# One PSUM ring, v projected ahead of k, q kept for the first attention block, attention in four stages between the FFN's tiles

## The chip, the cores and the metric

One core of a Trainium2 chip. The time is device microseconds of one execution of the program; the profile is one execution recorded by the hardware profiler. The engines are TensorE (PE), VectorE (DVE), ScalarE (ACT), GpSimd (POOL) and SyncE (SP, which only issues loads and stores here; ACT issues some too). Each engine runs its own queue in order, and waits on semaphores for the others.

## The reference

A transformer block over x of 2048 rows by 640: linear attention with a learned softmax feature map (32 heads of 20), then a gated FFN of 1536, both behind a layernorm and with a residual. All arrays are bf16.

```python
qkv = split(layernorm(x) @ wqkv)                    # q, k, v: 32 heads of 20
pq, pk = q @ w_phi[h], k @ w_phi[h]                 # 20 x 20 for each head
phi_q = concat(softmax(pq), softmax(-pq))
phi_k = concat(softmax(pk), softmax(-pk))
kv, z = sum_s(phi_k * v), sum_s(phi_k)
o = (phi_q @ kv) / (phi_q @ z + 1e-6)
h = x + o @ wo
out = h + (gelu(layernorm(h) @ w_gate) * (layernorm(h) @ w_up)) @ w_down
```

## The kernel before

The 2048 rows are 16 tiles of 128 rows, in 4 blocks of 4 tiles. The kernel has two phases, each with its own SBUF and PSUM pools.

Phase 1 (lines 93 to 281). `fold` multiplies w_phi into the weights of k and q (`Wk2`, `Wq2`): it transposes the raw weights piece by piece (tile `tp`, copied to `WT`), and multiplies each by block diagonals `BD` (L149, L156, PSUM `wa` and `wb`). `ln1` normalises a tile, transposes it on PE (L169) and stores it in `LN1T`. For each tile `k_tile` projects k (L183, PSUM `pk`), takes exp(pk) and exp(-pk) on ACT (`E`, L187), sums them by head on DVE (`sk`, L190) and takes reciprocals (`rs`, L192). `v_tile`, one tile behind, projects v (L200, `pv`), and scales it by `rs` into `vt`: one sign on DVE out of PSUM (L206), the other on POOL out of an SBUF copy `vS` (L210), with a column of `rs` (L213). `kv_half` sums over 8 tiles (L223, `kvp`); its second run adds the first half (`acc`) and masks into `KV` (L232, L233). `q_chunk` projects one 128-column piece of q for a block (L243, `pq`) and takes both exps into `Eq`: 20 chunks, from tile 6 on one per tile, the rest behind the second `kv_half`.

Phase 2 (from L286). Its pools open when phase 1 is over, and its weights `Wg`, `Wu`, `Wd` are loaded then. `attn(b, tl)` handles one tile: 14 matmuls of `Eq` with `KV` (L313, `ab`), ACT copies to `AB` (L320), then a chain on DVE: `pr`, `den`, `rd`, two `w`, two `tt` (L333, L336), `o` (L340). PE transposes o (L343, `tpo`), ACT copies it to `oT`, PE multiplies by `Wo` (L350, `po`), DVE adds x into `h_b` (L352), takes statistics, POOL computes `ve` and `rstd` (L87, L89), DVE writes `ln` (L356), PE transposes it (L359, `tpl`) and ACT copies it to `LN2T`. `ffn(b)` has 12 steps of gate and up (L367, L371; gelu on ACT, product `GT` on DVE), then for each of 4 tiles 24 matmuls of down (L381, `pd`), the residual on DVE (`y`, L384) and a store. The program writes attn(0, 0..3), then for each block attn of the next block and ffn of this one.

The order on each engine is not quite that of the code: the framework's scheduler moves instructions forward where their operands allow, within the buffers that the pools hold. PSUM in phase 2 is five one-bank buffers for `ab`, `gp`, `up`, two for `po` and `pd`, one for transposes.

Of the kernel before, what the change touches and what calls it, by code (L numbers as in the profile page):

```python
# [17 lines left out]
def kernel(  # L18
# [50 lines left out]
    nhalf = const.tile([P, 1], F32, name="nhalf")  # L69

    mid_cm = tc.tile_pool(name="mid", bufs=1, side="right")
    mid = mid_cm.__enter__()
    LN1T = [mid.tile([P, NC, 512], BF16, name=f"LN1T{b}") for b in range(NB)]
    Wq2 = mid.tile([P, NC, D], BF16, name="Wq2")
# [4 lines left out]
    def ln_stats(pool, halves, tag):  # L79

        stats = small(pool, [P, 2, nc.vector.BN_STATS_DIM], "stats" + tag)
        for i, hv in enumerate(halves):
            nc.vector.bn_stats(stats[:, i, :], hv)  # L83
        mv = small(pool, [P, nc.vector.BN_AGGR_DIM], "mv" + tag)
        nc.vector.bn_aggr(mv, stats)  # L85
        ve = small(pool, [P, 1], "ve" + tag)
        nc.gpsimd.tensor_scalar_add(ve, mv[:, 1:2], EPS)  # L87
        rstd = small(pool, [P, 1], "rstd" + tag)
        nc.gpsimd.tensor_tensor(rstd, ve, nhalf, op=ALU.pow)  # L89
        return mv, rstd  # L90


    with tc.tile_pool(name="p1", bufs=1) as p1, \
            tc.tile_pool(name="p1t", bufs=1, space=PSUM) as psT, \
            tc.tile_pool(name="p1k", bufs=1, space=PSUM) as psK, \
            tc.tile_pool(name="p1v", bufs=1, space=PSUM) as psV, \
            tc.tile_pool(name="p1q", bufs=2, space=PSUM) as psQ, \
            tc.tile_pool(name="p1a", bufs=1, space=PSUM) as psA:
        raw_k = p1.tile([P, NC, D], BF16, name="raw_k")
# [24 lines left out]
        nc.gpsimd.affine_select(out=m6, in_=m6, pattern=[[Dh, 6]], compare_op=ALU.is_ge,
                                fill=0.0, base=Dh - 1, channel_multiplier=-1)

        nc.vector.tensor_tensor(
            BD[0:120, 0:5], wphi[0:120, 0:5, None, :].to_broadcast([120, 5, 6, Dh]),
            m6[0:120, None, :, None].to_broadcast([120, 5, 6, Dh]), ALU.mult)
        nc.vector.tensor_tensor(  # L130
            BD[0:40, 5, 0:2], wphi[0:40, 5, None, :].to_broadcast([40, 2, Dh]),
            m6[0:40, 0:2, None].to_broadcast([40, 2, Dh]), ALU.mult)

        def fold(raw, W2):

            WT = p1.tile([P, 6, D], BF16, name="WT", bufs=1)
            for g, (o, n) in enumerate(FG):
                tp = psT.tile([P, NC, P], BF16, name="tp", tag="T")
                for c in range(NC):
                    nc.tensor.transpose(tp[0:n, c, :], raw[:, c, o:o + n], ident)  # L140
                if g % 2 == 0:
                    nc.vector.tensor_copy(WT[0:n, g, :], tp[0:n])
                else:
                    nc.scalar.copy(WT[0:n, g, :], tp[0:n])
            for c in range(NC):
                wa = psQ.tile([P, 512], F32, name="wa", tag="Q")
                for g in range(4):
                    o, n = FG[g]
                    nc.tensor.matmul(wa[:, o:o + n], lhsT=WT[0:n, g, c * P:(c + 1) * P],  # L149
                                     rhs=BD[0:n, g].rearrange("p a b -> p (a b)")[:, 0:n],  # L150
                                     start=True, stop=True)
                nc.scalar.copy(W2[:, c, 0:480], wa[:, 0:480])
                wb = psQ.tile([P, 512], F32, name="wb", tag="Q")
                for g in range(4, 6):
                    o, n = FG[g]
                    nc.tensor.matmul(wb[:, o - 480:o - 480 + n], lhsT=WT[0:n, g, c * P:(c + 1) * P],  # L156
                                     rhs=BD[0:n, g].rearrange("p a b -> p (a b)")[:, 0:n],
                                     start=True, stop=True)
                nc.vector.tensor_copy(W2[:, c, 480:640], wb[:, 0:160])

        def ln1(t):
            b, tl = divmod(t, 4)
            xt = x_sb[b][:, tl, :]
            mv, rstd = ln_stats(p1, [xt[:, 0:HD], xt[:, HD:D]], "1")
            ln = p1.tile([P, D], BF16, name="ln", bufs=3)
            nc.vector.tensor_scalar(ln, xt, mv[:, 0:1], rstd, op0=ALU.subtract, op1=ALU.mult)
            tp = psT.tile([P, NC, P], BF16, name="tp", tag="T")
            for c in range(NC):
                nc.tensor.transpose(tp[:, c, :], ln[:, c * P:(c + 1) * P], ident)  # L169
# [255 lines left out]
```

## Time and profile before

| | us |
|---|---|
| median of 3 runs | 373.04 (371.33 to 373.2) |
| the profiled execution, its own time | 372.27 |
| its span, first to last instruction | 370.2 |
| PE busy in the span | 313.7 (85%) |
| DVE busy | 206.0 (56%) |
| ACT busy | 148.6 (40%) |
| POOL busy | 58.7 (16%) |
| mean granted PE clock | 0.945 |

How to read it: a row of the stages gives each engine's busy time in a stretch; a row of the waits gives who idled for whom. PE's busy time is inflated where the granted clock is low, since the same matmul then takes longer. The chain that ended last consists of PE for 61% and of DVE for 22%.

### The profile page before, as it was taken

The page shows a single profiled execution, that of the slowest core. Times are in us where ns is not written, and L with a number is a line of the kernel's source. Part 1 is how long each engine was busy: PE and PEld are TensorE (multiplying, and loading weights), DVE is VectorE, ACT ScalarE, POOL GpSimd, SP SyncE. Part 2 cuts the span into 40 slices and gives each one's busy share as a digit, 9 for nine tenths or more (in the row PEclk, how much of TensorE's full clock was granted, in tenths as well). Part 3 has the DMA queues.
Part 4 walks back from the last instruction along what each step waited for, and adds up shares of the span by engine and source line. Part 5 has one row for each costly group of instructions (what it writes and reads, how often), then busy time and mean ns, then how long its engine had stood idle before and what let it go on. Part 6 is the DMA issues. An engine that isn't in the chain of part 4 may idle for free.

```text
span 370.2 us, 5473 instructions
## 1 busy us (share of the span) xinstructions
PE 313.7 (85%) x2163; PEld 191.1 (52%) x2188; DVE 206.0 (56%) x454; ACT 148.6 (40%) x260; POOL 58.7 (16%) x121
## 2 busy tenths in 40 slices
PE   0278999999999765468899979989988989999996
PEld 0156766776665443234445754444764444754464
DVE  4728899546652877835443277743359743332232
ACT  1056877778767542332431054233045233013200
POOL 4604365324410000001000001010001010000000
PEclk9989999999999866559999989999999999999999
DMA  8900000000004930000000100000010000010001
GB/s 262 372 6 4 2 0 3 0 2 2 0 0 123 397 122 1 0 2 0 0 3 0 55 18 2 0 0 2 35 38 0 2 0 3 35 37 0 0 19 54
DMA packets 9202, 14.79 MB, mean 40 GB/s; under 512 B 1113, under 2 KB 7385, under 8 KB 9177
## 3 DMA queue, kind: packets, MB, share of 16 engines
q1 hardware_dynamic: 6544, 11.96, 9.1%
q10 hardware_dynamic: 2633, 2.48, 2.0%
q8 instruction: 17, 0.28, 0.3%
q14 instruction: 8, 0.07, 0.1%
HBM read 11.82 MB, written 2.62 MB: 39 GB/s over the span
## 4 chain that ended last, share of the span: by engine, by line
PE 61%; DVE 22%; ACT 5%; DMA 4%; issue 4%; POOL 4%; ACTq 0%; POOLq 0%; DVEq 0%
PE pd L381 14%; PE gp L367 9%; PE up L371 9%; PE po L350 5%; PE pv L200 4%; PE pk L183 4%; DVE stats L83 4%; DMA Wv<-in_A_wqkv_dram 4%; PE pq L243 4%; PE kvp L223 3%; DVE h_b L352 3%; POOL rstd L89 2%; DVE ln L356 2%; DVE sk L190 2%; PE tpl L359 2%
## 5 line engine op out<-in xcount | busy, mean ns | idle before, releaser
L367 PE MATMUL gp<-LN2T,Wg 128*128 128x512 bf16 x229 | 61.9, 386 | 0.9 <-issue 0.4
L371 PE MATMUL up<-LN2T,Wu 128*128 128x512 bf16 x236 | 60.9, 379 | 0.2
L374 ACT ACTIVATE g<-gp 128x512 bf16<-128x512 f32 x48 | 28.7, 598 | 79.8 <-PE gp L367 74.0
L375 DVE TENSOR_TENSOR GT<-up,g 128x512 bf16<-128x512 f32 x48 | 32.8, 684 | 43.9 <-PE up L371 43.9
L381 PE MATMUL pd<-Wd,GT 128*128 128x320 bf16 x384 | 52.8, 299 | 0.0
L381 PEld LDWEIGHTS <-GT 128*128 128x128 bf16 x384 | 37.6, 98 | 15.2
L87 POOL TENSOR_SCALAR ve<-mv 128x1 f32<-128x1 f32 x32 | 7.9, 250 | 210.7 <-DVE mv L85 185.0
L320 ACT COPY AB<-ab 128x484 f32<-128x484 f32 (+1 forms) x48 | 23.0, 569 | 38.1 <-PE ab L313 27.5
L371 PEld LDWEIGHTS <-Wu 128*128 128x128 bf16 x240 | 23.3, 98 | 25.5
L367 PEld LDWEIGHTS <-Wg 128*128 128x128 bf16 x240 | 23.4, 99 | 24.2 <-issue 1.1
L384 DVE TENSOR_TENSOR y<-pd,h_b 128x320 bf16<-128x320 f32 x32 | 15.7, 492 | 35.3 <-PE pd L381 35.3
L350 PE MATMUL po<-Wo,oT 128*128 128x320 bf16 x160 | 31.8, 360 | 2.4 <-ACT oT L345 2.4
L200 PE MATMUL pv<-Wv,LN1T 128*128 128x320 bf16 x160 | 26.5, 309 | 3.9 <-DMA Wv<-in_A_wqkv_dram 2.9
L190 DVE TENSOR_REDUCE sk<-E 128x64 f32<-128x1280 bf16 x16 | 23.7, 1479 | 9.2 <-ACT E L187 9.1
L183 PE MATMUL pk<-Wk,LN1T 128*128 128x320 bf16 x160 | 26.4, 301 | 1.1 <-ACT E L187 1.1
L350 PEld LDWEIGHTS <-oT 128*128 128x128 bf16 x160 | 17.3, 115 | 17.0 <-ACT oT L345 7.7
L360 ACT COPY LN2T<-tpl 128x640 bf16<-128x640 bf16 x16 | 11.1, 692 | 37.1 <-PE tpl L359 37.1
L352 DVE TENSOR_TENSOR h_b<-po,x_sb 128x320 bf16<-128x320 f32 x32 | 15.4, 485 | 17.7 <-PE po L350 17.4
L359 PE MATMUL tpl<-ident,ln 128*128 128x128 bf16 x80 | 8.0, 238 | 19.3 <-DVE ln L356 19.3
L210 POOL TENSOR_TENSOR vt<-vS,rs 128x640 bf16<-128x640 bf16 x16 | 20.4, 1273 | 24.6 <-ACT vS L204 20.9
L243 PE MATMUL pq<-LN1T,Wq 128*128 128x512 bf16 x90 | 23.6, 379 | 0.4
L187 ACT ACTIVATE E<-pk 128x640 bf16<-128x640 f32 x32 | 21.0, 702 | 6.6 <-PE pk L183 6.2
(72 smaller groups left out, 400.6 us busy)
## 6 DMA issues: line engine op xcount, KB each, us to landing
out_dram<-y SPq DMA_DIRECT2D x16, 160.0 KB, 1.8
x_sb<-in_A_x_dram SPq DMA_DIRECT2D x3, 640.0 KB, 7.7
Wg<-in_B_w_gate_dram SPq DMA_DIRECT2D x1, 1920.0 KB, 7.8
Wu<-in_B_w_up_dram SPq DMA_DIRECT2D x1, 1920.0 KB, 12.3
Wd<-in_B_w_down_dram SPq DMA_DIRECT2D x1, 1920.0 KB, 18.0
raw_k<-in_A_wqkv_dram ACTq DMA_DIRECT2D x1, 800.0 KB, 11.8
Wv<-in_A_wqkv_dram ACTq DMA_DIRECT2D x1, 800.0 KB, 15.0
raw_q<-in_A_wqkv_dram ACTq DMA_DIRECT2D x1, 800.0 KB, 16.2
```

The lines of the kernel that those rows point to most:

```text
L183: nc.tensor.matmul(pk[:, u, 0:HD], lhsT=lnT(t, c), rhs=Wk2[:, c, u * HD:(u + 1) * HD], start=(c == 0), stop=(c == NC - 1))
L190: nc.vector.reduce_sum(sk, E.rearrange("p s (h f) -> p (s h) f", f=Dh), axis=AX.X)
L200: nc.tensor.matmul(pv[:, u, 0:HD], lhsT=lnT(t, c), rhs=Wv[:, c, u * HD:(u + 1) * HD], start=(c == 0), stop=(c == NC - 1))
L243: nc.tensor.matmul(pq, lhsT=Wq2[:, kc, c * P:(c + 1) * P], rhs=LN1T[b][:, kc, :], start=(kc == 0), stop=(kc == NC - 1))
L320: nc.scalar.copy(AB[:, :, h0:h1, :].rearrange("p s h f -> p s (h f)"), ab[:, :, 0:(h1 - h0) * KC])
L350: nc.tensor.matmul(po, lhsT=oT[:, c, :], rhs=Wo[:, c, u * HD:(u + 1) * HD], start=(c == 0), stop=(c == NC - 1))
L352: nc.vector.tensor_tensor(ht[:, u * HD:(u + 1) * HD], po, x_sb[b][:, tl, u * HD:(u + 1) * HD], ALU.add)
L367: nc.tensor.matmul(gp, lhsT=Wg[:, c, f * P:(f + 1) * P], rhs=LN2T[b][:, c, :], start=(c == 0), stop=(c == NC - 1))
L371: nc.tensor.matmul(up, lhsT=Wu[:, c, f * P:(f + 1) * P], rhs=LN2T[b][:, c, :], start=(c == 0), stop=(c == NC - 1))
L374: nc.scalar.activation(g, gp, ACTF.Gelu_apprx_tanh)
L375: nc.vector.tensor_tensor(GT[:, f, :], up, g, ALU.mult)
L381: nc.tensor.matmul(pd, lhsT=GT[:, f, tl * P:(tl + 1) * P], rhs=Wd[:, f, u * HD:(u + 1) * HD], start=(f == 0), stop=(f == NF - 1))
```

## The change

- Pools: one PSUM ring of three two-bank buffers (`gtile`) for every matmul result of the whole program, and two one-bank buffers for transposes. Wg and Wu stand in SBUF from the start and load behind Wo; Wd loads into memory that E and vt leave.
- Loads: x's first tile, Wv, x's rest of block 0, raw_k, raw_q on SP's queue; ACT's issues only w_phi.
- v first: `v_tile` runs four tiles ahead of `k_tile` and leaves v in `vS` (6 buffers); `k_tile` scales it, DVE now reading SBUF. LN in pairs of tiles. `BD` is made by POOL in six instructions in place of two on DVE.
- kv sums over three groups of 6, 5 and 5 tiles; all five column pieces of one sign share one ring buffer.
- q in pairs of chunks, exps of 1024 columns: three pairs in the loop, seven between the stages of the first attention block.
- Attention in four stages: `attn0` to `o`, `attn1` transposes o, `attn2` to ln, `attn3` transposes ln; `weave` puts them between units of other work. One `tt` is POOL's. h is written over x.
- Gate and up of a step share one ring buffer; down of a tile fills one, with one `y`.

```diff
+    psG = ctx.enter_context(tc.tile_pool(name="psG", bufs=3, space=PSUM))
+    psT = ctx.enter_context(tc.tile_pool(name="psT", bufs=2, space=PSUM))
...
+    KG = [range(0, 6), range(6, 11), range(11, 16)]
...
+    def gtile(name):
+        return psG.tile([P, 2, 512], F32, name=name, tag="G")
...
+    def v_tile(t):
+        pv = proj(t, Wv, "pv")
+        vS[t] = p1.tile([P, D], BF16, name="vS", bufs=6)
+        nc.scalar.copy(vS[t].rearrange("p (u f) -> p u f", u=2), pv)
+
+    def k_tile(t):
+        pk = proj(t, Wk2, "pk")
...
+        vt = ev.tile([P, 2, H, VC], BF16, name="vt", bufs=8)
+        for s, eng in ((0, nc.vector), (1, nc.gpsimd)):
+            eng.tensor_tensor(
+                vt[:, s, :, 0:Dh], vS[t].rearrange("p (h f) -> p h f", f=Dh),
+                rs[:, s * H:(s + 1) * H, None].to_broadcast([P, H, Dh]), ALU.mult)
...
+    def q_pair(j):
+
+        pq = gtile("pq")
+        for i in range(2):
+            b, c = divmod(2 * j + i, NC)
...
+        nc.scalar.activation(Eq[j][:, :, 0, :], pq, ACTF.Exp)
+        nc.scalar.activation(Eq[j][:, :, 1, :], pq, ACTF.Exp, scale=-1.0)
+
+    ln1([0])
+    ln1([1])
+    ln1([2, 3])
+    block_diagonals()
+    v_tile(0)
+    v_tile(1)
+    fold(raw_k, Wk2)
+    v_tile(2)
+    v_tile(3)
+    fold(raw_q, Wq2)
...
+    for t in range(NT):
+        if t % 2 == 0 and t + 4 < NT:
+            ln1([t + 4, t + 5])
+        k_tile(t)
+        if t + 4 < NT:
+            v_tile(t + 4)
+        for k in range(len(KG) - 1):
+            if t == KG[k][-1] + 1:
+                kv_group(k)
+        if t in (11, 13, 15):
+            q_pair(qdone)
+            qdone += 1
+    kv_group(len(KG) - 1)
...
+        for s, eng in ((1, nc.gpsimd), (0, nc.vector)):
+            eng.tensor_tensor(
+                tt[:, s].rearrange("p (h f) -> p h f", f=Dh), AB[:, s, :, s:s + Dh],
+                w[:, s, :, None].to_broadcast([P, H, Dh]), ALU.mult)
...
+    def gate_up(b, f):
+        gu = gtile("gu")
+        for i, W in ((0, Wg), (1, Wu)):
...
+        gt = p2.tile([P, 512], BF16, name="GT", bufs=NF + 2)
+        nc.vector.tensor_tensor(gt, gu[:, 1, :], g, ALU.mult)
...
+    def weave(units, stages):
+
+        stages = sorted(stages, key=lambda x: x[0])
+        for i, (fn, *args) in enumerate(units):
+            while stages and stages[0][0] <= i:
+                _, g, *a = stages.pop(0)
+                g(*a)
+            fn(*args)
+        for _, g, *a in stages:
+            g(*a)
+
+    ATT = (attn0, attn1, attn2, attn3)
+    weave([(q_pair, j) for j in range(qdone, len(Eq))],
+          [(tl + d, ATT[i], 0, tl) for tl in range(4) for i, d in enumerate((0.3, 2.2, 3.1, 5))])
+    for b in range(NB):
+        units = [(gate_up, b, f) for f in range(NF)] + [(down, b, tl) for tl in range(4)]
+        stages = []
+        if b + 1 < NB:
+            stages = [(3 * tl + d, ATT[i], b + 1, tl) for tl in range(4) for i, d in enumerate((0.3, 2.2, 3.1, 5))]
+        weave(units, stages)
```

What the engines' queues make of it, at three places. First, the start, on ACT's queue before (the last row is its first work behind the loads):

```order
L107 DMA wphi<-in_A_w_phi_dram 120x5x20
L108 DMA wphi<-in_A_w_phi_dram 40x20
L109 DMA raw_k<-in_A_wqkv_dram 128x5x640
L111 DMA Wv<-in_A_wqkv_dram 128x5x640
L113 DMA raw_q<-in_A_wqkv_dram 128x5x640
L170 ACT_TABLE_LOAD
```

and on SP's queue now:

```order
L131 DMA x_sb_64<-in_A_x_dram 128x640
L132 DMA Wv<-in_A_wqkv_dram 128x5x640
L133 DMA x_sb_64<-in_A_x_dram 128x1920
L134 DMA raw_k<-in_A_wqkv_dram 128x5x640
L135 DMA raw_q<-in_A_wqkv_dram 128x5x640
L137 DMA x_sb_65<-in_A_x_dram 128x2560
```

The three large weights moved from a queue of their own into the one that loads x, and Wv from behind raw_k to ahead of it.

Second, ACT in the first attention block, before (a number behind a name is the buffer's, so the same number is the same tile; AB_1585 is tile 0's, AB_1660 tile 1's, AB_1735 tile 2's):

```order
L245 ACTIVATE Eq3_68<-pq_1547 128x512
L246 ACTIVATE Eq3_68<-pq_1547 128x512
L320 COPY AB_1585<-ab_1586 128x2x242
L320 COPY AB_1585<-ab_1592 128x2x242
L320 COPY AB_1585<-ab_1600 128x2x220
L320 COPY AB_1660<-ab_1661 128x2x242
L320 COPY AB_1660<-ab_1667 128x2x242
L320 COPY AB_1660<-ab_1675 128x2x220
L320 COPY AB_1735<-ab_1736 128x2x242
L320 COPY AB_1735<-ab_1742 128x2x242
L320 COPY AB_1735<-ab_1750 128x2x220
L345 COPY oT_1626<-tpo_1620 128x640
```

and now (AB_1430 is tile 1's, AB_1485 tile 2's, oT_1477 and oT_1555 are those of tiles 0 and 1):

```order
L266 ACTIVATE Eq4_77<-pq_1417 128x2x512
L267 ACTIVATE Eq4_77<-pq_1417 128x2x512
L335 COPY AB_1430<-ab_1431 128x2x242
L335 COPY AB_1430<-ab_1444 128x2x220
L110 COPY oT_1477<-tpo_1478 128x640
L335 COPY AB_1430<-ab_1431 128x2x242
L266 ACTIVATE Eq5_78<-pq_1464 128x2x512
L267 ACTIVATE Eq5_78<-pq_1464 128x2x512
L335 COPY AB_1485<-ab_1486 128x2x242
L335 COPY AB_1485<-ab_1499 128x2x220
L110 COPY oT_1555<-tpo_1556 128x640
```

Before, all exps of q stood ahead of the first AB; now a pair of them stands between one tile's AB and the next one's.

Third, DVE in an FFN block, behind one tile's `po`, now:

```order
L371 TENSOR_TENSOR x_sb_65<-po,x_sb_65 128x640
L98 BN_STATS stats_1865<-x_sb_65 128x6 x2
L99 BN_AGGR mv_1864<-stats_1865 128x2
L339 TENSOR_TENSOR pr<-AB 128x64
L341 TENSOR_TENSOR den<-pr 128x32
L374 TENSOR_SCALAR ln_1873<-x_sb_65,mv_1864,rstd_1871 128x640
L343 RECIPROCAL rd<-den 128x32
L345 TENSOR_TENSOR w<-AB,rd 128x32
L346 TENSOR_TENSOR w<-AB,rd 128x32
L349 TENSOR_TENSOR tt<-AB,w 128x640
L353 TENSOR_TENSOR o<-tt 128x640
L389 TENSOR_TENSOR GT<-gu,g 128x512 x3
```

and before, in the block at 161.7 us:

```order
L352 TENSOR_TENSOR h_b<-po,x_sb_59 128x320
L83 BN_STATS stats_1944<-h_b 128x6
L352 TENSOR_TENSOR h_b<-po,x_sb_59 128x320
L83 BN_STATS stats_1944<-h_b 128x6
L85 BN_AGGR mv_1947<-stats_1944 128x2
L356 TENSOR_SCALAR ln_1953<-h_b,mv_1947,rstd_1951 128x640
L375 TENSOR_TENSOR GT<-up,g 128x512
L340 TENSOR_TENSOR o<-tt 128x640
L375 TENSOR_TENSOR GT<-up,g 128x512
```

Before, most of the next block's chain to o had been done ahead of this block; now each tile's chain stands whole between two tiles' products GT, and the second tt is on POOL's queue.

More of the change, by code (lines that the diff above doesn't have):

```diff
@@ L73, with transpose_to @@
+    def transpose_to(dst, src, name):
+        tp = psT.tile([P, NC, P], BF16, name=name, tag="T")
+        for c in range(NC):
+            nc.tensor.transpose(tp[:, c, :], src[:, c * P:(c + 1) * P], ident)
+        nc.scalar.copy(dst, tp)
+    mid = ctx.enter_context(tc.tile_pool(name="mid", bufs=1, side="right"))
     LN1T = [mid.tile([P, NC, 512], BF16, name=f"LN1T{b}") for b in range(NB)]
     Wq2 = mid.tile([P, NC, D], BF16, name="Wq2")
[L76 to L77 removed]
```

516 lines of the change are left out of this document (226 added, 290 removed).

## The prediction

> **What bounds the kernel now.** I read the stages first, then what TensorE (PE) waited for, then single rows for prices. The stages, cut where one line takes over from another on PE (columns: stretch and length, busy time and instructions of each engine, granted PE clock, DMA share, GB/s):
>
> ```profile
> 0.00:17.30 17.30, 1.50 (x10) 1.07 (x11) 11.75 (x34) 1.98 (x2) 10.33 (x38) 1.00 0.92 315
> 17.30:96.90 79.60, 74.51 (x609) 52.60 (x616) 54.92 (x92) 58.65 (x103) 31.54 (x47) 0.98 0.02 7
> 96.90:118.30 21.40, 20.92 (x168) 13.27 (x169) 10.13 (x25) 13.82 (x25) 3.48 (x4) 1.00 0.08 15
> 118.30:161.70 43.40, 24.37 (x187) 16.12 (x185) 30.68 (x87) 17.48 (x35) 3.14 (x8) 0.65 0.34 130
> 161.70:214.20 52.50, 49.27 (x290) 27.17 (x293) 22.15 (x45) 13.55 (x21) 3.12 (x8) 0.96 0.03 10
> 214.20:271.70 57.50, 52.90 (x351) 30.31 (x353) 31.85 (x76) 17.97 (x32) 3.57 (x8) 0.97 0.04 12
> 271.70:327.90 56.20, 51.38 (x349) 29.67 (x352) 31.78 (x76) 18.00 (x32) 3.57 (x8) 1.00 0.04 12
> 327.90:366.90 39.00, 38.81 (x214) 20.92 (x214) 12.23 (x20) 7.17 (x12) 0.00 (x0) 1.00 0.05 18
> 366.90:370.20 3.30, 0.00 (x0) 0.00 (x0) 0.49 (x1) 0.00 (x0) 0.00 (x0) 1.00 0.14 50
> ```
>
> PE is the bound except in three places: before 17.3 us (loads), in the first attention block (118.3 to 161.7: 24.4 us busy at a granted clock of 0.65), and for a few us at the head of the blocks at 214 and 272. The waits say for whom (engine and line, released by, total, times, longest):
>
> ```profile
> PE pv L200 <- DMA Wv<-in_A_wqkv_dram: 2.9, 1, 2.9
> PE tpl L359 <- DVE ln L356: 19.3, 16, 3.6
> PE tpo L343 <- DVE o L340: 4.6, 3, 1.6
> ```
>
> PE waits for attention's two serial chains, AB to o and po to ln. I name four terms: A up to the end of the last k projection (96.9 now), B from there to the first gate matmul (161.7; 64.8 long), C the four FFN blocks (205.2), D the tail (3.3). Outside the span lie 372.27 - 370.2 = 2.07 us. The change leaves the matmuls as they are, so PE's work is priced by full-rate rows:
>
> ```profile
> 85.27 1.36 PE pv L200 x10
> 89.06 0.28 PE tp L169 x5
> 104.56 0.68 PE L223 MATMUL kvp<-vt,E 128*128 128x147 bf16 x8
> 105.08 0.81 PE L243 MATMUL pq<-LN1T,Wq 128*128 128x512 bf16 x3
> 127.91 0.87 PE L313 MATMUL ab<-KV,Eq 128*128 128x88 bf16 x14
> 194.67 1.08 PE gp L367 x5
> 201.15 13.04 PE pd L381 x96
> ```
>
> That is 1.36 us per projected tile, 0.28 per transposed tile, 0.065 per kvp (eight start 0.52 before the next matmul), 0.22 per 512-wide matmul, 0.87 per ab tile, 13.0 per down.
>
> **Term A: loads, v first, folds, groups.**
>
> ```profile
> 3.27 0.89 DVE L83 BATCH_NORM_STATS2 stats<-x_sb 128x6 f32<-128x320 bf16 x2 [3.27 <-DMA x_sb<-in_A_x_dram]
> x_sb<-in_A_x_dram SPq DMA_DIRECT2D x1, 160.0 KB, 2.5
> GB/s 262 372 6 4 2 0 3 0 2 2 0 0 123 397 122 1 0 2 0 0 3 0 55 18 2 0 0 2 35 38 0 2 0 3 35 37 0 0 19 54
> 17.34 2.02 PE L200 MATMUL pv<-Wv,LN1T 128*128 128x320 bf16 x7 [2.85 <-DMA Wv<-in_A_wqkv_dram]
> ```
>
> Wv moves from behind raw_k on ACT's queue to second place on SP's, so its load stops being late. The three x tiles behind it land 800 KB later: 1.44 MB at the 0.372 MB/us of the page's second slice, plus the 2.5 us that the first small load took, is 6.4 us. What is late next is the LN chain: the order has PE do three transposed tiles before the first v, and GpSimd (POOL) squeezes the masks and the new block diagonals between the variances. Adding up those short instructions I get the third LN tile at 12.1 and the first v matmul at 12.7. From there PE work up to the last k tile: 32 projections 43.5, 16 LN tiles 4.5, folds 12 x 0.28 plus 60 narrow ones of about the same pitch 6.7, 110 kvp 7.2, 20 q matmuls 4.3: 66.2 us. Seven microseconds of waits come on top: 1.7 for a cold first stretch (below), 3.5 for copies between the folds' transposes and products, 2 for the first kvp of a group. **A = 12.7 + 66.2 + 7.2 = 86.1.** DVE could take over as the bound: it is busy 11.75 + 54.92 = 66.7 us up to 96.9 now, for nearly the same work, and begins at 3.3, so it needs till 70 at least and has 16 us for its own waits. Ends: 80.6 with no fold or group wait, 95 if the waits stay as now (the present A has about 69 us of PE work behind 13.7, so 14 of waits).
>
> **Term B: q kept, first attention block woven.** Three q pairs are now done before T0 (the end of the last k tile), seven after. First KV must be finished; prices of that chain:
>
> ```profile
> L187 ACT ACTIVATE E<-pk 128x640 bf16<-128x640 f32 x32 | 21.0, 702 | 6.6 <-PE pk L183 6.2 <-PE kvp L223 0.3
> L190 DVE TENSOR_REDUCE sk<-E 128x64 f32<-128x1280 bf16 x16 | 23.7, 1479 | 9.2 <-ACT E L187 9.1
> L192 DVE RECIPROCAL rs<-sk 128x64 f32<-128x64 f32 x16 | 8.7, 543 | 0.3
> L210 POOL TENSOR_TENSOR vt<-vS,rs 128x640 bf16<-128x640 bf16 x16 | 20.4, 1273 | 24.6 <-ACT vS L204 20.9 <-DVE rs L192 3.7
> L213 POOL CAST vt<-rs 128x64 bf16<-128x64 f32 x16 | 7.7, 483 | 4.4 <-DVE rs L192 3.2 <-PE pk L183 1.2
> L233 DVE TENSOR_TENSOR KV<-kvs,hmask 128x147 bf16<-128x147 f32 (+1 forms) x10 | 3.2, 319 | 0.3
> ```
>
> ACT has a q pair's two exps (about 1.0 each, by E's 702 ns for 640 elements) ahead of the last two E, so the last E ends at T0+2.3; sum 1.5, two reciprocals 1.1 and POOL's two vt with casts, taking turns with DVE's, 3.9: T0+8.8. The 43 kvp that stand behind take 2.8 (11.6); a q pair's rest fills 1.5; meanwhile DVE adds and masks, five instructions per sign, about 2.0 by the 319 ns for 147 elements: KV is whole at 14.9, and tile 0's AB lies in SBUF at 17.4. Then each tile runs this chain:
>
> ```profile
> 214.45 1.47 ACT AB L320 x3
> 215.94 0.25 DVE pr L324
> 218.80 0.42 DVE o L340
> 219.26 0.45 PE L343 MATMUL tpo<-ident,o 128*128 128x128 bf16 x5 [1.52 <-DVE o L340]
> ```
>
> 3.34 us from the last copy (215.92) to tpo with both tt on DVE. One tt now goes to POOL. Do the two overlap? These rows say not:
>
> ```profile
> 225.62 0.77 DVE L333 TENSOR_TENSOR tt<-AB,w 128x640 bf16<-128x640 f32 x1
> 225.79 0.68 POOL L87 TENSOR_SCALAR ve<-mv 128x1 f32<-128x1 f32 x1 [36.21 <-DVE mv L85]
> 233.90 0.22 POOL L87 TENSOR_SCALAR ve<-mv 128x1 f32<-128x1 f32 x1 [6.78 <-DVE mv L85]
> ```
>
> A ve of 0.22 us took 0.68 and ended 0.08 us after the tt it met. So I cost DVE's 0.73 and POOL's 1.27 (vt's price, same element count) one after the other: 3.34 - 0.73 + 1.27 = 3.9 us; side by side it would be 3.2. The Trainium skill, "SBUF — State Buffer", section "Who interferes with whom", says that a VectorE instruction with two SBUF inputs contends with a GpSimd one that reads SBUF, and that the loser fully blocks; that rule speaks against this edit, and the trace agrees with 0.68 against 0.22.
>
> The order gives PE, per tile: tpo, three q matmuls, six ab, then the q pair's rest, and the next tpo waits: 0.3 + 0.65 + 0.4 + copy 0.75 + 3.9 = 6.0 us, of which PE works 3.3 (2.16 of it q). Tpo of tiles 0, 1, 2: 21.3, 27.3, 33.3. From there the queue holds 12.7 us of PE work (ab's rest, three q pairs, three po, five transposes); tile 1's ln is 1.9 late, since DVE does o of tile 3 first, and the last ln takes its whole chain:
>
> ```profile
> 230.11 1.53 PE L350 MATMUL po<-Wo,oT 128*128 128x320 bf16 x10
> 235.29 0.45 PE L359 MATMUL tpl<-ident,ln 128*128 128x128 bf16 x5 [0.42 <-DVE ln L356]
> ```
>
> about 3.6 from po's end, of which 3.3 is bare; with the last copy 0.9: 33.3 + 12.7 + 1.9 + 3.3 + 0.9 = 52.1. The clock is the last item:
>
> ```profile
> 214.20:219.80 5.60, 3.87 (x61) 3.17 (x59) 4.17 (x13) 3.86 (x9) 0.00 (x0) 1.00 0.08 29
> 219.80:223.50 3.70, 3.48 (x14) 1.75 (x12) 2.48 (x7) 2.53 (x6) 0.00 (x0) 0.54 0.00 0
> ```
>
> After 5.6 us at 69% busy the clock was 0.54 for 3.7 us: 1.7 us lost. B's cycles are at 55%, so I charge two such stretches, 3.4. The Trainium skill, "TensorE: Matmul & The Clock Gate", section "HAM oscillation — how this bites in real kernels", wants no idle gap over about 3.4 us. By that rule B's gaps of 2.7 cost nothing and the sum would be 347. The trace differs: the longest gap ahead of that stretch was the 1.52 us before 219.26. **B = 55.5** (64.8 now). Ends: 48 (full clock, tt side by side), 64.8 (chains as now).
>
> **Term C: attention in stages in the FFN.** Block 3 has no attention and stays 39.0. Attention's PE work per tile is 0.87 + 0.28 + 1.36 + 0.28 = 2.8, so a dense block is 39.0 + 11.2 = 50.2. Between two po PE has ab, gate_up, tp2, gate_up, tpo, gate_up. Tp2 comes 0.87 + 2.16 = 3.0 after po but ln needs 3.6: 0.55 wait. Then DVE finishes o: AB is whole at 2.0, ln ends at 3.5, rd, two w, tt, POOL's tt and o end at 6.7, PE comes at 6.0: 0.75 wait. Behind o stand three GT on DVE, and the three-buffer ring waits for GT; they end 1.5 us before po or ab needs the buffer. So 1.3 per tile, 0.65 in a block's first: 4.5 per block. **C = 3 x 54.7 + 39.0 = 203.1.** Ends: 194 (0.4 per tile, no wait for o), 211.5 (three blocks like the present 57.5).
>
> **Costed at nothing:** Wg and Wu load behind Wo at the start, over 100 us ahead of use; Wd waits on SP for the last kvp, with only output stores behind it, and has 27 us of block 0 before down; fewer, larger ACT copies; LN in pairs. If Wd had no such cover it would cost its load, some 18 us. D: one y of 640 for two of 320 ends 0.3 later: **3.6**.
>
> **Sum:** 86.1 + 55.5 + 203.1 + 3.6 + 2.07 = 350.4 against 372.27 profiled; the median of the runs is 0.77 above that, so I say 351 against 373.
>
> **Rivals.** (1) *Full overlap* (0.20): POOL's tt and the clock cost nothing, and the waits in C halve: 350.4 - 7 - 5 = 338, 339 on the median. For it: the clock stayed 1.00 behind a similar head at 272. Against: ve's 0.68, and 0.54 behind the head at 214. The Trainium skill's "TensorE: Matmul & The Clock Gate" stands on this rival's side for the clock alone. (2) *A's gain missing* (0.15): DVE's 66.7 us, its waits and the coupling through six vS buffers hold PE, A = 95: 359, 360 on the median. For it: DVE starts its sums only after both folds, some 30 us in. Against: 54.92 busy of 79.6 now. (3) *The weave does not do what it says* (0.08): q runs out before the chains, B stays 64.8: 360, 361 on the median. The order, which has q matmuls up to the last po, speaks against it. (4) *Slower* (0.06): the woven waits lower the clock. From a wait of about 1.5 us in each tile, a 1.7 us stretch like 219.80 to 223.50 follows each one: C + 12 x (1.7 + 0.5), and B loses 6 more: 383, 384 on the median. The 1.00 of 271.70 to 327.90, with waits under 1 us, speaks against. It decides from 22.6 / 12 = 1.9 us per tile on, if A and B gain what I say.
>
> **Numbers.** My forecast has 0.51. Its own ends, taken together as unrelated errors (5.5, 7.5 and 9 below; 9, 9 and 8.5 above), give -13 and +15; the range 336 to 364 holds rivals 1 to 3 as well and leaves (4) and tails out. About 0.5% is what a measurement of this kernel can tell from no change. Faster 0.93, same 0.02, slower 0.05.
>
> **What would show it.** A: first v matmul near 12.7, last k near 86. B: first gate 52 to 57 behind, gaps of 2 to 3 us ahead of tpo, some clock below 0.8. C: three blocks near 54.7, waits of tp2 for ln and tpo for o, POOL's tt or DVE's visibly longer when they meet. A B over 62, or blocks over 57, would make the prediction wrong.

## The result, and the profile after

The changed kernel takes 358.08 us (median of 4 runs, 356.74 to 359.78) against 372.19 for the kernel before beside it: a ratio of 0.963, 95% interval 0.956 to 0.969. Its profiled execution took 356.91 us, its span 355.2, at a mean granted clock of 0.980. The forecast was 351, with a range of 336 to 364. One of the four executions in experiment 12 took 1092.73 us and is left out of its ratio.

The stages of the changed kernel, cut as the stages of before (the same columns). The first cut is the first v matmul, the second the first k projection, the third the end of the last one, then the first gate matmul of each block and the end of the last down:

```profile
0.00:14.46 14.46, 1.93 (x16) 1.41 (x17) 5.97 (x17) 2.67 (x3) 7.64 (x35) 1.00 0.91 309
14.46:31.30 16.84, 15.40 (x178) 12.17 (x177) 13.94 (x40) 11.32 (x18) 3.74 (x8) 1.00 0.84 321
31.30:87.80 56.50, 52.71 (x462) 39.56 (x461) 44.73 (x64) 39.79 (x63) 30.22 (x33) 1.00 0.01 1
87.80:143.22 55.42, 37.31 (x263) 23.28 (x266) 34.28 (x66) 28.06 (x41) 16.73 (x20) 0.91 0.11 36
143.22:200.71 57.49, 52.85 (x348) 29.91 (x352) 33.33 (x63) 19.73 (x33) 8.26 (x12) 0.97 0.03 10
200.71:256.60 55.89, 51.21 (x350) 29.56 (x352) 34.14 (x64) 18.48 (x32) 8.26 (x12) 1.00 0.04 13
256.60:312.50 55.90, 51.20 (x350) 29.55 (x352) 34.15 (x64) 18.48 (x32) 8.26 (x12) 1.00 0.04 12
312.50:351.70 39.20, 39.04 (x215) 20.97 (x215) 11.60 (x16) 7.17 (x12) 0.00 (x0) 1.00 0.05 18
```

| term | before | forecast | after |
|---|---|---|---|
| A, to the end of the last k projection | 96.9 | 86.1 | 87.8 |
| B, from there to the first gate matmul | 64.8 | 55.5 | 55.4 |
| C, the four FFN blocks | 205.2 | 203.1 | 208.5 |
| D, the tail | 3.3 | 3.6 | 3.5 |
| outside the span | 2.07 | 2.07 | 1.71 |

So all of the gain is in A and B (9.1 and 9.4 us), and C lost 3.3. But part of B's gain is work that was handed to C. The attention that is written with the first FFN block has 56 ab matmuls; the kernel before did them all ahead of that block. Now they stand in it, so that it has 348 matmul records in place of 290, and takes 57.5 us in place of 52.5. The next two blocks got shorter (57.5 to 55.9, 56.2 to 55.9). B and C together gained 6.1.

PE's waits of the changed kernel (engine and line, released by, total, times, longest):

```profile
PE tpo L109 <- DVE o L353: 11.3, 15, 2.5
PE kvp L235 <- POOL vt L226: 8.6, 5, 3.0
PE ab L331 <- ACT AB L335: 6.5, 12, 0.7
PE tp L109 <- DVE ln L374: 6.0, 5, 3.2
```

The third stood in the kernel before only once (0.5 us), and no term of the prediction held it: six of ab's 14 matmuls write the second bank of a two-bank buffer, and they wait until ACT has copied the first. The two tt of the attention, as groups and in one tile (start, length, engine and line):

```profile
L349 DVE TENSOR_TENSOR tt<-AB,w 128x640 bf16<-128x640 f32 x16 | 29.8, 1861 | 0.5
L349 POOL TENSOR_TENSOR tt<-AB,w 128x640 bf16<-128x640 f32 x16 | 21.0, 1315 | 68.8 <-DVE w L346 68.8
...
206.48 1.27 POOL L349 TENSOR_TENSOR tt<-AB,w 128x640 bf16<-128x640 f32 x1 [13.12 <-DVE w L346]
206.50 1.93 DVE L349 TENSOR_TENSOR tt<-AB,w 128x640 bf16<-128x640 f32 x1
```

DVE starts 0.02 us after POOL and ends 0.68 us behind it, though such a tt takes it 0.82 with no POOL beside it (run 1): it was held up for about 1.1 of POOL's 1.27 us, and the pair lasts 1.95.

In a full tile of the second FFN block the chain looks like this:

```profile
211.53 1.52 PE L368 MATMUL po<-Wo,oT 128*128 128x320 bf16 x10
213.99 0.42 PE L331 MATMUL ab<-KV,Eq 128*128 128x44 bf16 x6 [0.49 <-ACT AB L335]
219.79 0.45 PE L109 MATMUL tpo<-ident,o 128*128 128x128 bf16 x5 [0.59 <-DVE o L353]
222.24 1.52 PE L368 MATMUL po<-Wo,oT 128*128 128x320 bf16 x10
```

From the add behind po (213.09) to the end of o (219.73) DVE idles only 0.57 us, for POOL's rstd. Tpo follows at once and the next po 2.45 us later, so this chain sets the 10.71 us from po to po; the wait for AB lies beside it.

The granted clock, in the three stretches where it fell:

```profile
97.50:102.70 5.20, 5.14 (x42) 5.07 (x43) 1.44 (x4) 0.00 (x0) 0.00 (x0) 0.56 0.00 0
111.75:118.20 6.45, 4.78 (x29) 2.56 (x31) 3.56 (x7) 3.13 (x5) 1.27 (x1) 0.74 0.00 0
143.20:147.00 3.80, 3.78 (x11) 1.35 (x11) 0.00 (x0) 1.27 (x1) 0.00 (x0) 0.57 0.00 0
```

The first is the sum over kv at the end of the k loop, the second lies behind the first tpo, the third at the head of the first FFN block, behind a wait of 3.25 us for the last ln.

### The profile page after: what moved, and what is told of

It reads as the page before. It is cut to its first block, busy times and chain, and to the rows that moved or that the text cites. A ratio compares the mean times of both kernels' runs of the same rounds, so it can differ in the third digit from the quotient of the medians.

```text
span 355.2 us, 5377 instructions
## 1 busy us (share of the span) xinstructions
PE 301.7 (85%) x2165; PEld 186.4 (52%) x2188; DVE 213.0 (60%) x392; ACT 145.7 (41%) x230; POOL 83.1 (23%) x131
## 4 chain that ended last, share of the span: by engine, by line
PE 51%; DVE 30%; POOL 7%; ACT 5%; issue 4%; DMA 2%; SPq 0%; POOLq 0%; DVEq 0%; ACTq 0%
PE gu L384 15%; PE pd L396 12%; DVE tt L349 8%; DVE stats L98 5%; PE po L368 5%; PE pv L200 5%; PE pk L200 4%; DVE x_sb L371 3%; PE kvp L235 3%; POOL rstd L103 3%; PE pq L264 2%; DVE o L353 2%; DVE ln L374 2%; DMA x_sb<-in_A_x_dram 2%; PE tpo L109 2%
## 5 line engine op out<-in xcount | busy, mean ns | idle before, releaser
L387 ACT ACTIVATE g<-gu 128x512 bf16<-128x512 f32 x48 | 28.7, 597 | 93.8 <-PE gu L384 93.8
L384 PE MATMUL gu<-LN2T,Wg 128*128 128x512 bf16 x223 | 59.4, 384 | 1.6 <-ACT LN2T L110 0.8
L384 PE MATMUL gu<-LN2T,Wu 128*128 128x512 bf16 x240 | 60.2, 382 | 0.1
L389 DVE TENSOR_TENSOR GT<-gu,g 128x512 bf16<-128x512 f32 x48 | 32.1, 687 | 47.0 <-ACT g L387 47.0
L200 PEld LDWEIGHTS <-LN1T 128*128 128x128 bf16 x320 | 31.3, 99 | 12.1
L349 POOL TENSOR_TENSOR tt<-AB,w 128x640 bf16<-128x640 f32 x16 | 21.0, 1315 | 68.8 <-DVE w L346 68.8
L223 POOL TENSOR_TENSOR vt<-vS,rs 128x640 bf16<-128x640 bf16 x16 | 27.7, 1733 | 24.3 <-DVE rs L220 21.3
L400 DVE TENSOR_TENSOR y<-pd,x_sb 128x640 bf16<-128x640 f32 x16 | 13.2, 823 | 33.7 <-PE pd L396 33.7
L98 DVE BATCH_NORM_STATS2 stats<-x_sb 128x6 f32<-128x320 bf16 x64 | 27.8, 474 | 7.1 <-DMA x_sb<-in_A_x_dram 6.5
L109 PE MATMUL tp<-ident,ln 128*128 128x128 bf16 x160 | 14.4, 231 | 18.6 <-DVE ln L188 12.5
L349 DVE TENSOR_TENSOR tt<-AB,w 128x640 bf16<-128x640 f32 x16 | 29.8, 1861 | 0.5
```

The source lines that it names most:

```text
L98: nc.vector.bn_stats(stats[:, i, :], xt[:, i * HD:(i + 1) * HD])
L200: nc.tensor.matmul(ps[:, u, 0:HD], lhsT=lnT(t, c), rhs=W[:, c, u * HD:(u + 1) * HD], start=(c == 0), stop=(c == NC - 1))
L223: eng.tensor_tensor(vt[:, s, :, 0:Dh], vS[t].rearrange("p (h f) -> p h f", f=Dh), rs[:, s * H:(s + 1) * H, None].to_broadcast([P, H, Dh]), ...
L349: eng.tensor_tensor(tt[:, s].rearrange("p (h f) -> p h f", f=Dh), AB[:, s, :, s:s + Dh], w[:, s, :, None].to_broadcast([P, H, Dh]), ALU.mult)
L384: nc.tensor.matmul(gu[:, i, :], lhsT=W[:, c, f * P:(f + 1) * P], rhs=LN2T[b][:, c, :], start=(c == 0), stop=(c == NC - 1))
L387: nc.scalar.activation(g, gu[:, 0, :], ACTF.Gelu_apprx_tanh)
```

## The experiments

Each is the changed kernel with the edit shown, timed beside the kernel before; a ratio is to that kernel. Stage rows have the columns of above. The question of the first five is what C takes above its forecast, and for which of its two waits.

**1. Both tt on DVE.**

```diff
-        for s, eng in ((1, nc.gpsimd), (0, nc.vector)):
+        for s, eng in ((1, nc.vector), (0, nc.vector)):
```

> Both tt of the attention on DVE, none on POOL. Theory (the two tt shut each other out, so POOL's share lengthens the chain from w to o): DVE's tt falls from 1861 ns to about 810, the pair ends 1.6 us behind w instead of 1.95 to 2.0, o comes 0.4 to 0.5 us earlier in each of 16 tiles, the wait of tpo for o falls from 11.3 us in total to 4 or 5; C falls by 4 to 6 us, B by 1 to 2: 350 to 353 us against 358. Rival (POOL's share takes load off a DVE that is short of time): DVE gets 16 x 0.8 us more work between the products GT, gate and up wait for the ring, the blocks stay at 56 or grow: 358 to 364 us.

355.22 us (354.76 to 355.63), ratio 0.953 (0.949 to 0.957). Of this kernel, B, a full FFN block, and the end of one tile's chain:

```profile
90.34:141.06 50.72, 36.00 (x269) 22.57 (x266) 33.25 (x70) 28.04 (x40) 10.98 (x16) 0.93 0.12 40
199.38:254.87 55.49, 51.48 (x355) 29.54 (x352) 32.11 (x68) 18.47 (x32) 3.10 (x8) 1.00 0.04 13
...
226.26 1.55 DVE L349 TENSOR_TENSOR tt<-AB,w 128x640 bf16<-128x640 f32 x2
227.73 0.68 DVE L389 TENSOR_TENSOR GT<-gu,g 128x512 bf16<-128x512 f32 x1
228.33 0.48 DVE L353 TENSOR_TENSOR o<-tt 128x640 bf16<-128x640 bf16 x1
```

Two tt on one engine take 1.55 us, less than the pair's 1.95 on two. B fell by 4.7 us, more than foreseen: 3.4 of it is idle time of PE, the rest its busy time, at a clock of 0.93 in place of 0.91. But a block fell by 0.4 only, and C stayed at 208.5: the order that the scheduler chose for this kernel puts a product GT between tt and o. From the start of tt to that of o it is 2.07 us, against 2.03 in the changed kernel, so GT takes back what tt had freed. The theory of the shut-out holds; its expectation for C missed.

**2. ab's halves both multiplied before ACT copies.** The copies move behind the matmuls of both halves, in a loop of their own:

```diff
             for i in range(2 - v):
...
                     nc.tensor.matmul(
...
+            for i in range(2 - v):
+                h0 = UH * (2 * v + i)
+                h1 = min(h0 + UH, H)
                 nc.scalar.copy(AB[:, :, h0:h1, :].rearrange("p s h f -> p s (h f)"),
```

> Both halves of an ab buffer are multiplied before ACT copies either. Theory A (the wait of ab's second half for ACT's copy of the first, 12 x 0.5 us, is itself what C lost): that wait goes and C falls by 6 us, 352 us. Theory B (PE only comes 0.5 us earlier to tpo and waits there, since AB is whole no earlier: ACT's three copies stand back to back from the gelu ahead of them in either order): the 6.5 us of waits for AB go, the waits of tpo for o grow by nearly as much, C falls by less than 2 us, 357 to 358 us.

363.52 us (362.55 to 364.65), ratio 0.976 (0.971 to 0.980): slower than the changed kernel. Its waits, and a full block:

```profile
PE tpo L109 <- DVE o L356: 14.1, 12, 2.2
PE tp L109 <- DVE ln L377: 8.8, 14, 3.2
...
202.91:260.78 57.87, 51.45 (x355) 29.54 (x352) 34.03 (x64) 18.39 (x32) 8.44 (x12) 1.00 0.04 12
```

The 6.5 us of waits for AB are gone, and blocks got 2 us longer. So taking that wait away gave nothing: PE comes earlier to tp2 and tpo and waits there, as theory B said. But theory B's 357 to 358 missed too. DVE's chain from the add to the end of o grew from 6.64 to 7.34 us, because the scheduler changed its order: a GT stands between tt and o here as well (0.42 us more), and den stands behind ln, which waits for POOL's rstd (0.23 more).

**3. One more unit of cover.**

```diff
-            stages = [(3 * tl + d, ATT[i], b + 1, tl) for tl in range(4) for i, d in enumerate((0.3, 2.2, 3.1, 5))]
+            stages = [(min(3 * tl + d, 15), ATT[i], b + 1, tl) for tl in range(4) for i, d in enumerate((0.3, 3.1, 4.1, 7))]
```

> Only the due times in the FFN blocks: tpo and po one unit later, tp2 two, so three units of gate and up (6.5 us) stand between ab and tpo instead of two. Theory (C's excess is chain length against cover; the chain from ab's start to o is 6.2 us, PE work between was 5.2): the wait of tpo for o goes in the blocks (12 x 0.6 us), that of ab for AB goes partly: three blocks of 54.5 to 55.5 us instead of 55.9 to 57.8, C 204 to 206 against 208.5: 351 to 354 us. Rival (the order of DVE decides: po's add and ln of one tile now stand amid the next tile's chain): o or ln get later by 1 us in each tile, no gain or a loss, 357 to 362 us.

364.47 us (363.71 to 364.93), ratio 0.978 (0.974 to 0.982). The waits and a full block:

```profile
PE pd L396 <- DVE GT L389: 6.3, 3, 2.1
PE ab L331 <- DVE GT L389: 5.5, 6, 0.9
PE tpo L109 <- DVE o L353: 5.4, 3, 2.5
...
204.61:262.48 57.87, 52.30 (x355) 31.12 (x353) 33.80 (x64) 18.01 (x32) 8.21 (x12) 0.97 0.04 12
```

All that is left of tpo's wait are the three in B. But one GT stands between tt and o and two behind ln on DVE, ln waits 1.0 us for POOL's rstd, and what waits for GT is the ring (ab) and, at the block's end, down. The rival had the cause, DVE's order; the loss went beyond its 362.

**4. Edits 2 and 3 together.**

> Both of the edits before: ab's halves first, and three units of cover. Theory B of the second run (AB's wait and o's wait are one excess, seen at two places): now neither is left, 12 x 1.1 us go, three blocks near 51 to 53 us (dense is 50.2), C 194 to 199, 344 to 349 us. Theory A: the two gains are independent, so the sum of what the two runs gave by themselves. If something else sets the blocks (the granted clock, DVE), they stay above 54.

355.11 us (352.65 to 355.54), ratio 0.953 (0.948 to 0.958). A full block:

```profile
198.49:253.26 54.77, 50.63 (x354) 30.17 (x352) 33.85 (x64) 17.58 (x32) 8.22 (x12) 1.00 0.04 13
```

Each edit alone cost 2 us per block, both together gain 1.1. They are not independent, so theory A is out. But 54.77 is not the 51 to 53 of theory B either: PE still waits 6.2 us for GT at the heads of down, and a GT still stands between tt and o.

**5. Both tt on DVE, and o ahead of GT.** The edit of run 1, and every GT queued behind the last o:

```diff
+        last[0] = nc.vector.tensor_tensor(o, tt[:, 0], tt[:, 1], ALU.add).ins
...
+        with tc.issue_after(last[0]):
+            nc.vector.tensor_tensor(gt, gu[:, 1, :], g, ALU.mult)
```

> Both tt on DVE as in the first run, and no product GT may be issued on DVE between a tile's tt and its o. Theory (in the first run the FFN blocks gained only 0.4 us each because the order put one GT of 0.69 us between tt and o, which ate the 0.5 us that the tt had freed): now o comes 0.6 us earlier in each of 12 tiles, the wait of tpo for o in the blocks falls from 0.5 to 0.1 or less, the two full blocks take 53.2 to 54 us against 55.5: 349 to 351 us against 355. Rival (GT, now later, is what the three-buffer ring waits for): gate and up wait for GT 0.5 us per tile instead, the blocks stay at 55 to 56, 355 us.

350.74 us (350.19 to 351.54), ratio 0.941 (0.939 to 0.942). The same place of a tile, and a full block:

```profile
225.63 1.55 DVE L349 TENSOR_TENSOR tt<-AB,w 128x640 bf16<-128x640 f32 x2
227.22 0.49 DVE L353 TENSOR_TENSOR o<-tt 128x640 bf16<-128x640 bf16 x1
227.63 1.46 DVE L390 TENSOR_TENSOR GT<-gu,g 128x512 bf16<-128x512 f32 x2
...
199.47:253.29 53.82, 51.29 (x354) 29.65 (x352) 32.47 (x68) 18.11 (x32) 3.11 (x8) 1.00 0.04 13
```

The profile shows no wait of tpo for o any more, and a block is 2.1 us shorter than in the changed kernel. The changed kernel has o ahead of GT too, so in this chain only the engine of one tt differs, and o starts 1.59 us behind the start of tt in place of 2.03. This shows for the full blocks what the wait for o was: a tile's chain on DVE, from po's add over ln, w and tt to o, sets the cycle, and the tt pair is its piece that the change made longer. It doesn't bring C to its forecast: C is 205.4, and the first block, at 58.5, did not gain.

**6. x ahead of Wv; kv sums tile by tile.** Two edits in two stages:

```diff
-    nc.sync.dma_start(Wv, w_v[:, :, 2 * D:3 * D])
     nc.sync.dma_start(x_sb[0][:, 1:4, :], x_v[:, 1:4, :])
+    nc.sync.dma_start(Wv, w_v[:, :, 2 * D:3 * D])
...
-            for c in range(NC):
-                for t in tiles:
+        kvps = [gtile("kvp") for s in range(2)]
+        for t in tiles:
+            for s in range(2):
+                for c in range(NC):
```

> Two edits in two stages, against the changed kernel: x's rest of block 0 loads ahead of Wv, and the kv sums run tile by tile over both signs instead of column piece by column piece. Theory for A: x's rest lands near 5.5 us instead of 7.65, the first v matmul starts at 12.3 to 12.8 instead of 14.3, A ends 1.5 to 2 us earlier. Theory for B (30 of the 50 last kvp wait in PE's queue behind a matmul whose vt is last, then run at a clock of 0.56): they are worked off before, 20 are left behind the last vt, KV is whole 13 to 14.5 us behind the last k instead of 17.4, and B takes 51 to 53 us instead of 55: 353 to 355 us. Rival for B: two of the three ring buffers are now held while the last vt comes, q pairs come later by as much, and what is won at KV is given back before the first gate: B stays at 55, 356 to 357 us.

350.58 us (349.95 to 352.53), ratio 0.942 (0.939 to 0.946). The k loop, B, and the last kv sums of this kernel:

```profile
30.57:82.99 52.42, 52.42 (x464) 39.41 (x462) 45.09 (x65) 39.70 (x63) 30.77 (x33) 1.00 0.01 2
82.99:135.82 52.83, 35.37 (x268) 21.97 (x266) 34.47 (x66) 28.25 (x41) 16.68 (x20) 0.92 0.12 38
...
90.71 1.43 PE L235 MATMUL kvp<-vt,E 128*128 128x147 bf16 x10 [3.33 <-POOL vt L226]
92.69 1.43 PE L235 MATMUL kvp<-vt,E 128*128 128x147 bf16 x10 [0.56 <-POOL vt L226]
```

In the k loop PE does not wait at all: 52.42 busy of 52.42, against 52.71 of 56.50. The first v matmul starts at 12.15 in place of 14.46, but the folds' copies give back most of it, and the first k projection is only 0.7 earlier. A ends at 83.0, 4.8 earlier where 1.5 to 2 were expected; 4.1 of it come in the k loop, from the kv order. B: KV is whole at 97.7, 14.7 behind the last k (17.4 before the edit), and B is 2.6 shorter, so the rival for B is out.

**7. No q kept between the stages.**

```diff
-    weave([(q_pair, j) for j in range(qdone, len(Eq))],
+    for j in range(qdone, len(Eq)):
+        q_pair(j)
+    weave([],
```

> Against the changed kernel: all seven kept q pairs are written ahead of the first attention block instead of between its stages. Theory of the prediction (the kept q fills the waits for the chains): without it the chains stand bare, B goes towards 64.8, 360 to 368 us. Rival (the DVE chain of about 6.3 us per tile sets B in either case, and the q pairs that stand ahead of the last tpo delay it): KV at T0 + 17 to 20, four chains of 6.3, then 5 to 7 us for the last ln: B 50 to 55, 353 to 358 us.

364.50 us (363.47 to 365.26), ratio 0.978 (0.976 to 0.980). B, and the q pairs in it:

```profile
89.55:149.25 59.70, 39.61 (x269) 23.71 (x267) 33.22 (x66) 28.41 (x41) 16.56 (x20) 0.87 0.11 34
...
103.69 14.62 PE L264 MATMUL pq<-LN1T,Wq 128*128 128x512 bf16 x67
```

B is 59.7 against 55.4: the kept q is worth 4.3 us there. The time lies in the theory's range, but B came out between the two expectations: the chains take most of B either way, and the q pairs hold up the first ab when they stand ahead of it (28.6 us behind the last k, 16.2 in the changed kernel).

**8. No weave.**

```diff
-        weave(units, stages)
+        weave([], stages)
+        weave(units, [])
```

> Against the changed kernel: the four stages of the next block's tiles are written ahead of each FFN block in one piece, not between its units. Theory (the ring of three and the order of the code let nothing of gate and up slip between the stages): DVE's work of 6.5 to 7 us per tile stands nearly bare, three blocks of 68 to 76 us instead of 56 to 58: 395 to 415 us. Rival (the scheduler interleaves as it did in the kernel before, whose blocks took 52.5, 57.5 and 56.2 us with attention written in one piece): blocks of 55 to 58, 355 to 362 us, and the weave is worth nothing.

438.69 us, a single execution. A full block:

```profile
269.51:353.38 83.87, 60.92 (x353) 34.48 (x352) 35.04 (x64) 18.92 (x32) 8.34 (x12) 0.81 0.02 8
```

83.9 us instead of 55.9, more than the theory said; the clock, at 0.81, is part of it. With one ring of three buffers and this order of the code the chains stand bare. So the weave does what it says within this design; but the kernel before, with attention written in one piece and its own five-buffer pool, had blocks of 56.2 and 57.5 us without it.

**9. Edits 5 and 6 together.**

> Three edits together: both tt on DVE, no GT between tt and o, x ahead of Wv, kv sums tile by tile. Theory (the gains lie in different stages and add up): A near 83 us, B 55.4 less 5 and less 2.5, so 47 to 49, the blocks as where o came first (53.8 each, the first 57 to 58.5), C 204 to 206: 340 to 343 us. Rival (what one stage wins by a shorter wait the next loses: B's chains stand barer when KV comes earlier): B stays at 50 to 53: 344 to 347 us.

342.04 us (341.69 to 342.31), ratio 0.918 (0.914 to 0.922). B and the first two blocks:

```profile
83.24:132.56 49.32, 35.49 (x269) 22.03 (x267) 33.42 (x70) 28.03 (x40) 10.97 (x16) 0.91 0.13 41
132.56:189.81 57.25, 53.74 (x352) 30.49 (x352) 31.67 (x67) 19.39 (x33) 3.11 (x8) 0.96 0.03 10
189.81:243.64 53.83, 51.30 (x355) 29.65 (x352) 32.47 (x68) 18.11 (x32) 3.12 (x8) 1.00 0.04 13
```

The gains add up: A 83.2, B 49.3, C 204.1. This version beats both kernels, by 31 and 16 us.

**10. Edits 5, 6 and 2 together.**

> As the run with three edits, and both halves of an ab buffer multiplied before ACT copies either (0.43 us of waits per tile in the blocks). Theory (PE reaches tpo with no slack already, so the next wait is that for o): the wait for AB goes, that for o or for ln comes back with 0.3 to 0.6 us, the blocks stay within 0.7 us of 53.8, the median within 1.5 us of the run with three edits, more likely above it. Rival (the wait for AB is now the only one left in the blocks): 12 x 0.43, 335 to 338 us.

343.60 us (343.49 to 344.69), ratio 0.923 (0.920 to 0.927), 1.6 us above run 9. A full block and the longest of its waits:

```profile
189.99:244.53 54.54, 51.28 (x355) 29.63 (x353) 32.44 (x68) 18.31 (x32) 3.15 (x8) 1.00 0.04 13
...
PE tp L109 <- DVE ln L379: 1.1, 4, 0.3
PE tpo L109 <- DVE o L358: 0.8, 3, 0.3
```

As in run 2, the wait for AB goes and others come in its place, all for DVE; here o stands ahead of GT.

**11. Edits 5 and 6, and both vt on DVE.** In `k_tile`:

```diff
-        for s, eng in ((0, nc.vector), (1, nc.gpsimd)):
+        for s, eng in ((0, nc.vector), (1, nc.vector)):
```

> As the run with three edits, and both vt of the k loop on DVE, POOL only casts. Theory (in the k loop DVE is nearly the bound, busy 45.1 of 52.4 us, and it is POOL that is held up there, 1.73 us for 1.27, in the shadow): 16 x 0.83 us more make DVE the bound, A grows by 4 to 8 us, B by -1 to +1: 344 to 350 us. Rival (the shut-out costs here as it does between the two tt): kvp waits less, A is the same or 1 to 2 us shorter, KV comes 1 us earlier: 338 to 341 us.

344.92 us (342.47 to 345.70), ratio 0.925 (0.920 to 0.930), 2.9 above run 9. The k loop:

```profile
31.49:92.47 60.98, 55.08 (x464) 39.95 (x462) 54.17 (x78) 39.79 (x63) 17.33 (x22) 0.97 0.00 1
```

DVE is busy 54.2 of 61.0 us, and A ends 9.2 later, more than the 4 to 8 expected; B is 3.5 and the first block 1.9 shorter, which was not expected. The same kind of split that costs time in the attention gains 2.9 us in all here: in the k loop DVE is nearly the bound, and the engine that is held up is POOL (its vt takes 1733 ns in the changed kernel, 1273 before).

**12. v behind k again** (folds first, raw_k loaded ahead, on the changed kernel).

```diff
-    nc.sync.dma_start(Wv, w_v[:, :, 2 * D:3 * D])
+    nc.sync.dma_start(raw_k, w_v[:, :, D:2 * D])
     nc.sync.dma_start(x_sb[0][:, 1:4, :], x_v[:, 1:4, :])
-    nc.sync.dma_start(raw_k, w_v[:, :, D:2 * D])
+    nc.sync.dma_start(Wv, w_v[:, :, 2 * D:3 * D])
...
+        v_tile(t)
         vt = ev.tile([P, 2, H, VC], BF16, name="vt", bufs=8)
...
-    v_tile(0)
-    v_tile(1)
     fold(raw_k, Wk2)
-    v_tile(2)
-    v_tile(3)
...
-        if t + 4 < NT:
-            v_tile(t + 4)
```

> Against the changed kernel: v is projected behind k of the same tile again, the folds come first, and raw_k loads ahead of x's rest and Wv. Theory of the prediction (v ahead starts PE early and fills the folds' gaps, and vt finds v ready): the folds stand bare and 4 x 1.36 us of v come later, A ends 4 to 7 us later than 87.8 to 90.3, KV one projection later too: 362 to 367 us. Rival (the start waits for loads and LN in either case, and A's 9 us came from the single scaling of v in SBUF, LN in pairs and kv sums in three groups): A within 2 us, 357 to 360 us.

361.67 us (three executions 361.22 to 361.87), ratio 0.970 (0.966 to 0.975). Its last two projections and the rest up to the first gate (which starts at 146.80):

```profile
94.24 1.52 PE L200 MATMUL pk<-Wk,LN1T 128*128 128x320 bf16 x10
95.60 1.52 PE L200 MATMUL pv<-Wv,LN1T 128*128 128x320 bf16 x10
...
96.96:146.80 49.84, 34.83 (x268) 21.10 (x266) 29.85 (x63) 27.19 (x39) 13.58 (x16) 0.95 0.13 40
```

The last k ends at 95.6, 7.8 us later than 87.8: most of the 9.1 that A gained comes from v going first, with the order of loads and folds that belongs to it; this run doesn't part the three. But B, from the end of the last k, is 51.2 and not 55.4, since a projection of v again covers part of the chain behind the last k. So v first is worth 4 us in the profiles (3.6 in the medians), not 8.

## Why the prediction was right, and where it was off

The forecast of 351 was 7 us below the median and within its range; 22 us were forecast, 14 came. By the terms of the sum:

- **A (+1.7): the start was mis-sized.** x's three tiles landed at 7.65 us, not at 6.4, and the first v matmul stood at 14.46, not 12.7. The rest is 73.3 us against the 73.4 of the sum, by luck: PE was busy for 68.1 us, not 66.2, and idle for 5.2, where the sum had 7.2 of losses. The first kvp of a group waited 3.7 us, not 2, the folds' copies cost less than 3.5, and the 1.7 for a cold first stretch did not come: the clock was 1.00 from 14.46 to 87.8. Run 12 shows the step "v first" right for A, run 6 the load: with x ahead of Wv it landed at 5.1. The 95 of rival 2 did not come: DVE was busy 44.7 of the 56.5 us of the loop.
- **B (-0.1): right, in its parts too.** KV was whole at T0 + 17.4 against 14.9; but its kvp ran at 0.56, and 5.14 us at that clock are 2.3 lost; with 1.2 in the stretch behind the first tpo that is about the 3.4 us that the sum had put as a lump at the end. Tpo's cycles were 6.4 and 5.9 (said 6.0), the rest from the third tpo 19.1 (said 18.8). The chain from AB to tpo was 3.9, as priced with the two tt one after the other. Run 1 shows the alternative: with both on DVE B is 50.7. By the Trainium skill, "SBUF — State Buffer", section "Who interferes with whom", a VectorE instruction with two SBUF inputs contends with a GpSimd one that reads SBUF; that agrees with 1861 ns here against 816 with no POOL beside it (run 1). Run 7 shows the step "q kept" right in sign at 4.3 us, run 8 that of the weave, and B is not 64.8, so rival 3 is out.
- **C (+5.4): the term that was off.** A block with attention was priced at 54.7 and took 55.9, and 57.5 the first time. The steps held, their sizes did not quite. A tile's cycle from po to po was 10.71 us, against 10.6 by the sum (9.3 dense and 1.3 of waits): 0.4 over three tiles. The first tile's waits and the one for the last ln came to 1.1, not 0.65, and a block without attention took 39.2, not 39.0. The waits stood elsewhere than foreseen: 0.49 for AB, which was not in the sum at all, and 0.59 for o, where 0.55 for ln and 0.75 for o were expected. Runs 2 and 10 show that taking the wait for AB away gives nothing, run 5 that a shorter chain on DVE does. The first block's further 1.6 us fit its head, which ran at 0.57 for 3.8 us: the low clock was charged to B alone. By the prediction's own sign, blocks over 57, that block crossed the line.
- **Rival 1** (full overlap, 339) fell with the 1861 ns of tt and the three stretches of low clock. **Rival 4** (slower) was near in one respect: a tile lost 1.4 us (10.71 from po to po, 9.3 dense), of the 1.9 from which it decided. But the full blocks kept a clock of 1.00.

What was costed at nothing held: no load stands among PE's waits. What stays open: B, still 46 to 51 us in the runs with a shorter chain, and the first FFN block, 57 to 58.5 us in runs 5 and 9, were not taken apart further; and why the scheduler put GT ahead of o in runs 1 to 4 and not in the changed kernel was not looked into.

## What to carry to other kernels

When attention is woven into dense work, add up the whole serial chain of one tile on its slowest engine and compare it with the PE work between its stages: here a wait removed at one stage returned at the next, and what moved the time was a shorter chain together with an order that keeps other work out of it. More cover with such an order was not tried. Give an operation to a second engine where the first is the bound (vt in the k loop), not where both stand in one tile's chain (tt). In sums over tiles, order the matmuls so that what is ready runs before what waits: in run 6 that left no wait in the k loop.

## What the hardware showed beside that

Which of the two engines is held up is not fixed. In nearly every tile POOL's tt starts 0.02 us ahead and DVE's takes 1.93; in one tile of the first attention block of the changed kernel both are listed at 121.53, and there DVE's took 0.82 and POOL's 1.95.

The same wait is followed by a low clock in one execution and not in another. The sum over the first kv group, in the changed kernel and then in run 1, whose code is the same up to there:

```profile
54.58 3.83 PE L235 MATMUL kvp<-vt,E 128*128 128x147 bf16 x55 [2.10 <-POOL vt L226]
```

```profile
55.49 5.45 PE L235 MATMUL kvp<-vt,E 128*128 128x147 bf16 x55 [2.11 <-POOL vt L226]
...
56.00:60.00 4.00, 4.00 (x38) 4.00 (x36) 0.82 (x1) 0.85 (x2) 2.88 (x4) 0.57 0.00 0
```

A wait of 2.1 us, and then 55 matmuls at full clock in the one, 1.6 us longer in the other, with 4 us at 0.57. The loop from the first to the last k projection took 56.5 us in two profiles of this code and 58.1 in six. The Trainium skill, "TensorE: Matmul & The Clock Gate", section "What's actually happening", describes a free-running window of about 3.4 us in which activity is watched, so that the turning point depends on where in it the work falls. That agrees with two outcomes of one wait. The rule of the Trainium skill, same page, section "HAM oscillation — how this bites in real kernels", no idle gap over about 3.4 us, is kept by a gap of 2.11 us, and yet 4 us at 0.57 followed in run 1. Run 6, in which that wait is gone, had a clock of 1.00 throughout the loop, and so had run 9.
